# Normed rows through VectorE blocks and DRAM, LayerNorm sums on ScalarE, and masked blocks made differently, in a DeltaNet and Fourier-mixing kernel on one core

## The chip, the cores and the metric

The kernel runs on one core of a Trainium2 chip. Its time is the device time of one execution in microseconds. The median of the runs of the kernel before is 627.87 us. One execution was also taken by the hardware profiler, and every view of the profile below is of that one.

## The reference

Two blocks follow each other. The first is DeltaNet attention: four batches, eight heads, 768 tokens, head dimension 48, all float32. The second takes the heads side by side as 384 features, mixes tokens and features by two Fourier transforms, and adds a normalised two-layer network.

```python
k_n = k / (np.linalg.norm(k, axis=-1, keepdims=True) + 1e-06)
for t in range(S):
    y[:, :, t] = einsum('bhd,bhde->bhe', q[:, :, t], state)
    v_old = einsum('bhde,bhd->bhe', state, kt)
    state = state + bt * einsum('bhd,bhe->bhde', kt, vt - v_old)
x = y.transpose(0, 2, 1, 3).reshape(B, S, H * D)        # 4 x 768 x 384
u = x + real(fft(fft(x, axis=1), axis=2))
un = (u - mean(u)) / sqrt(var(u) + 1e-06)               # over the 384 features
out = u + maximum(un @ w_ch1, 0) @ w_ch2                # 384 -> 1536 -> 384
```

## The kernel before

**Attention.** The 24 units are pieces of 128 tokens of one batch (six to a batch, `T` = 0 to 5), each with all eight heads. Units are prepared in seven rounds. Rounds 0 and 1 (batch 0) go an early way of their own; the other five, of 4, 4, 4, 3 and 3 units, go through `prepare` and `consume`. For each unit TensorE turns keys and queries (`turn`, through line 353) and multiplies keys with keys and queries (`gram`). From the key products ScalarE and VectorE copy a diagonal part with a half mask into `lo` and join it with another part in `gd` (`ev_l`, `ev_g`, line 592). A round's `gd` is turned on VectorE into `rr` (line 643), inverted there row by row in sixty products and sums (`invert`, lines 936 and 941), scaled (line 950) and turned back (line 953). `blocks` then multiplies each unit's part of `gd` by a mask that keeps the upper triangle and the half it belongs to (line 963), turns 32-wide blocks (line 969), and the rest of the unit's inverse, its states and its outputs follow on TensorE (`quarters`, `ahead`, `step`, `outputs`).

**Mixing.** When a batch's six units are out, VectorE folds the rows (`folds`), TensorE does both transforms (`seq6`, `feat`), and VectorE adds and takes the LayerNorm statistics (lines 1515 and 1517). `normed` applies them to a 128 x 384 row tile `un` (VectorE, line 1539, or ScalarE, line 1537). There are six such tiles in a batch, two to a group `g`, twelve groups in all. Three TensorE transposes of 128 x 128 (line 353, tile `pm`) turn a tile, and one copy of 128 x 384 (line 359 on ScalarE or 361 on VectorE, `R<-pp`) brings it into `R0`, where the group's 256 tokens lie as [feature, token]. `R0` has places for two groups.

**Network.** `mlp` and `mlpw` read it from there as the moving operand of the first layer's products. `mlpw` uses a seven-product scheme for part of the work; its differences of 128 x 128 parts of the normed rows are made by VectorE at line 1728. Group (2,2) is worked in the last batch, after its attention.

**Order.** A string, `ORDER`, lists every piece of work in the order in which it is issued; each engine runs its own in that order. `issue` reads it. An entry has two characters for the piece, one for the engine if there is a choice, one for each new PSUM bank, and two more, for a DMA on SP with a size, that name the piece after which it is paced. An entry past the last piece is three characters: a group of dummy TensorE products (`fill`, lines 2172 and 2178). DMAs wait in SP's queue in the same manner: one that waits holds up those behind it.

```python
while place < len(text):
    i = take(2)
    if i >= len(self.ops):
        fill(i - len(self.ops), take(1))
        continue
    o, self.ins = self.ops[i], None
    e = o.engs[0] if len(o.engs) == 1 else ENGINES[take(1)]
    for b in o.new:
        b.slot = take(1)
    after = take(2) if o.kb and e == "SP" else i
```

Of the kernel before, what the change touches and what calls it, by code (L numbers as in the profile page):

```python
# [32 lines left out]
FOLD, SEQ, HOTG = 1, 10, 1  # L33
# [24 lines left out]
AGDAJDAKBAAAODAPBAEDARAWtGBAZAKAIDAMBAXAaAKABASACDAbGAAdCAcCAeBCAhGFAgBAfCAiANBA7AGAFBAUCA6A6AYAQBA4  # L58
AGATAjBMDBBNCAVAlAkAsAoADDAtBJEHBKCBLCAmAyAuAvGaAUAwBbA8ACA+CAxBPDEA9CA5AiBOCBQDCAQBCBCA2AzA0BmBnBqA
nBrBuBvA-FACoAGGbA0C8AFBRByApBzCzABBTB2CuAhDIAMAHDBACB3BBCBDA3C2A9B6A1ArB7HLBTBSAqBEBUHKBLtFHBVALDB+  # L60
BGtGHB-tGHBFCCtCHBHBaBWCDGjB-BIBcBdtGHBgCtAtCGBXBeCHBfDDFGCpDEGqAxDECCKtGCCqCCvCDDJABBhCLBiDKCBoCrHG
COGcBYBpCPCStGEBsCTG7DDC9EFBtGiBGCWtGABwCXHMBxtGACaB0CwCtGACbB1C+CCeCgCfCxABC0CB4DZCDXtGCDaCC3CDDcED
dDYCDeCCiB5ChDbCCsDfFDgHOGkC4CB8DhDjDiBZDkDlDmDFGHC5CDGmB9C6DoCCADpEDqDuCDNCpBjCBDtCDrCDsCDLCDDnCDvF
GzDjCyDwCEGrDgDxCDMC-ABCFCIDGCJCMDyCC1BDzCD0CD3GCD4CD1FED5CD6HDVDGD2CD7CD8DEGeD9CEAG6GmECCEDCEBFDEEG
yC0CNCQCRCUCVCYCZCcCdCjClCkEQCESCEOFRCETEERCEUEFCGdFTCFQEVCGfGgFVGC7CeCmFWEPCCnFUCFSBDBDBEWCEXEaEZEY
EbEcGsG8EdDABkEJFXCFYGELCEKCFZHDEBGhGlG0EMEgEGuENCEhEfCD+ABD-BGnGoFdDHDrG1FbEiCEwEkCElCFcFaFeFfEzCBl
EjCEGEeCGpDOBDPBEuCDEHCEIBEmEEvCEyCGtGvGwEnFiGFjFmBHSEDEpCEoCHTDAErCE2EqCEsABFkBExFEE0FnBG2E4CEtCE+A
BE1CFhBHCBkE5E7BE6BE8HUGdDQBFlCHVHVMYFcFgCHWHYHXHZE3CFoDE9CE-CFCHNFFCFECDRBHcEKFpMkBlG+G9G-FqBFtBHdE
kG3G4HAHfEvHPHQHaFDBCFGMLElFAFGFHCNJHEMKEsFLFBCFMBFrCFNCMIFbFsCFIFJCMZEoFOFPCFyFKCF0CGxFzEAHGHFFwFGH
eE2F1BHgF2FuBCHBF3CDSEoFxCMJFJHHHIHhHjFvCF4F6CG5HbF5CJNF7F8CDUEuF9CMlE7MmBDMoCF+GAFGF-CGEGFDCHiHkDTG  # L70
-JMGHBGBCMOFNMaFGMnCGGBMbCJOMwHhJPGIGCABGJCGDCGNGOCJQGKGPCHlJTJRHqF1JUHJHnFqHmHFGQHpHpH9FOMcCQPFLGRC
GLCJ3EFGMCGUGWCMpGHGVCHRJSJVGSABJWJZJcDWFsH1FNGTCH0JSJdJgMdCDMeJjHoHbHyHgQzJcMfGXHzMdHrFPMgM8GGJkGYC
GZCJ4MPMaJXJYJaJbJeJfJiJhMqH2JnH8GIJqHsMxGNJlJmJoH+MeHuJrIBJhMMJhJpJsJtHtMsHvHwH4M9JOJuBAJvJwJxCJyCM
jJ0CMiMhH3MrH5H6IAMaJ5J6CJ9CJ7BJ1CH-GVKADCKBJ8BHxKJAEMtKCKSGBMNF8QOJqJzCKKJ-CJ2CMvJ+BKDKTICMUGSKMKLM
yECH7KEKFM+DHNACIJIJM-CKNKbABIIJqKGMzCKHKVKOKcIKH2KIKPKkFDKtHEKeQbQbM0CKUKQKdKRIEKuM1BCK2IWJ4K3GIMIM
K5MuKWKlIDIFIGK4CM4K6AK7CIVMeILKIININIOQRMyKfKgKwNBDELHAIUKBM2QLIDIXK5KvIPM3KnIHNDKmQaM-KXM7IYIgKKNC
NEM6Q-Q-NGIQIRISIjKMNHLBGQyKCKYNINKIaIeKlLICNLIZKZIbIcLEFK8HITLFCM5NMNNIhM0NOQ0FANFNPIdQKM0IsM6KhK9C
KaNXLRItIDQcBCQeCIfIPQ2CIiKMIqIEIrKfNYNZNaNbNcNdK+HKoIkQ1CNRKiIlImInIoI3KeLKAKjKxKyKpK-CNeLADHLDKqI4
KlQ+NDIpLCCNfI5LHI2KhIuIZNgNhNiNjNkNlMVNCQdCNmNnKzNoIvK-NpJBJBLUI6LSFI8IwK0K1LTCQQIHQfBCQmIYJDJDIyQi
IxQhNqNrQnNqLGNsNQQNIbLVENtNuNvNwIzI0LJJAKpJEJEQgLLCQkNxI7RAAGNyI9I+QjNzLWCQMK1QoFEI1QlN0JFI9Q3BCRBC  # L80
I-LMQ7LXAN1N2N3N4Q4N5Q5Q8JCNRJGJHJJQ6QpCRLNSRCCN6KrKsJIJKJLLsQqCQrGFQvN7N8N9QsQuQtQwQxRDBCRGN+N-OARH
OBRERJOCLNLOLYCLZGQ9LbEFRFRIODRKOENVCMRLsRMOFRNROMSMSRPLaCLcBOGOHOILeRQOJOKLPMWQtRRMTMTRZRaOLOMLdCRb
ONRcRdOOReRfMQRAOPLhOQLfALtCRgLiBLgCOROSOTOUOVOwOWOxPOOXDOYCOyGLkNTCRhRiRjRkRlRmRnRoRpRqRrRsRtRuRvRw
RxOzCLjCLlAOZHO0BO2CPsLmCLnRyRzOcCRTOaCR0ObCOdCLuCR1MXMXO4CPPOeGAOfCDO3BPtPuHR2R3RUR4O1CR5R6R7R8PQBO
hCOiCPRBOjCOgCOkGLvLoNUCLpNWCLwAOlR9OmBCLqO5DEOnPvCLxCO6GHO9CO8COpFOoBOqO7CPSAR+R-SASBSCSDPWCPUCPwBO
-CDPTCPyCL0GO+CPAPCHPBCPVBOrADPzCPXFESEYiRTPxCL1CSFSGPDPEGHP0CYaOcPYBCOuQVPtPaCPbBOvSHSISJPGCPZCOtCL
yDQUOmLzCPFPHFPcCP1BCSKSLPJDGSMSNSOSPSQPISRSSSTP4CRSPdEFYjHBPNYbPQOsCPeP6CPfBYkCPgAPhP2EFYlCP5BPiABP
3CPMPjPLYtO-SUPkCYuHGYwCYvCLrPlCPKPmYmEFP7ABYxDCSVP8P+HYnYpP-YsYoP9CYzYqL2GHQSPLQTQTSWY0SXS1RVCQAABL
3ESYY1QBYyY2YrSZCYcP+QCCSaBS2PnFDPpRWBQFBCY4SWL4CZDPGQDAQESbEScBQIPoYdP7QJPqL5QGQHPrXhSeCSfCTSSdCY3S
gFESlCSjCShABY5CDSkBSiCY6BSmABY7CZEFEZFCSnSpCSoBS3DSqSrABZGCXiY8EFS4CStCS5CX8S8CY-SsY+ZHABX9TRZASuDZ  # L90
LSvS9CY9S7CZIZBS6BZPL8ZKTVZCZNTTS+DCZJS-ABTDCTBCTUXjEX+FZMQWY9ZOTACX-CXkCTEABTCCTFSwFCSxQZYySyTHETIT
GCTJABXlESzS0TKTLCTbYACTMFDTaTXTWTcTdTYYCCTQTPXnCL6ATOL9BXmCTNL7CYECTfTZTeThZQZRLQTkTgL-TiQYXlTjTnTq
TlTmTpTrXoCToTsTtL+CMCTuTvZSZTZUZVZdMADMBCZeZfMHTYT4AFZgQXQXZhZiRXCT5ZjT7BT9CTwBDZkXpCZXYDCT6CTxTzCT
yCZlT+CT1CT-BYBBXqEAT2CT0CZmZnZoXtCUKBDULUAFCYeMCZpZqXvCU9UBUUDEUMUNUOUCYfTuUDUVT3BT8CMDUeEFXrBCUPRY
CUEUWUFUXUQURXuCXwAUGUHMEUTMFUYUfZrUSXsCXxVIVJCUhUgZsUIZtUJYFFDYGGHYHCYJCXyBCVKEVEVLCUoAHYgMCZuYICVF
BZvUpVGGVHCUyEHVMGUZVAX0CVNCXzYKCZwZxU8ZyVSFZzVQVOZ0X3CBVPU+VTCUqUrUaUiUcVRVUX1DVCgMVIUjZ1X5CZ2UzUbV
WX4CUdVVVXZ3gSUTZ4UkZYU0Z5U-Z6Z7VDWEWFBX2U1Z8VYAHGVZFVaCVbZ9g1Z+VdUsVfVgCVhCVcZZCWGFZ-gzX6VeZaCaAUla
BVmVnEVkVoCVBaCX7ViVjaDaEVlVtYLDEaFaGaHaIaJWHCaKaLU2aMaNaOUmaPaQZWZbCVpVqYNCgTFCgUCVrUnYMVuBgVCVsaRa
SaTWIV0WJCWKFVvCaUaVVwVxWLCYOEgWBCgXaWaXaYaZYPVzgZVyYQEFYSCV2V1V4aaV5aba5a6YRWMDgaacbXV3a7EV9adFWNCY
VCDgYWOV7a8CYTEV8aeCYUWPafFagCa9BaiCV+a+CYWYYa-BahCYZajCYXWQWCV6gdgTWSEbABbBCakDFV-WAgNacbYgbapCWBWR  # L100
alCBamCbZHaqABWDWTBaoCanCarWUasCbCDFbGCbHCatCgeEGUtgfCauavABawbDEFggCaxBayCghABbFCbECaza0FCbIDEb1b2g
OV7gjbaBgla2a1UubJgkbbHgia4WYGAFbfCbKCgmbeBbdCWWWVgoVygpEDbLBa3gqBbcCbgHCgrCU3blCbMbkCgcgsDEgubNBCU4
U5gwWXgvgngtgygxg0g2WfUwbPCWZDWgEbjBg3g4g5bOWaCWbg6UvWcWhCbQBWdg7hCbhDCb3HbRhDYhg5bSEBMGWebWbiCb4CU6
# [2108 lines left out]
```

## Time and profile before

| | |
|---|---|
| runs | 625.07, 627.87, 3294.46 us; median 627.87 us |
| profiled execution | 629.74 us, its span 627.9 us |
| mean granted TensorE clock | 0.986 |
| TensorE busy | 603.0 us, 9722 products |
| VectorE busy | 533.7 us, 1477 instructions |
| ScalarE busy | 280.0 us, 790 instructions |
| DMA | 31.98 MB, mean 51 GB/s |

Busy time is a mean over stages. To about 100 us the attention of batch 0 is a chain of small steps beside the conversion of the weights; from then on attention of the next batch, mixing and network run beside each other, and from about 535 us only the network of the last batch is left. The 3294.46 us run is far from the other two, and the median doesn't feel it. Products overlap on TensorE, so the mean duration of one is longer than the time that it adds.

### The profile page before, as it was taken

The page shows a single profiled execution, that of the slowest core. Times are in us where ns is not written, and L with a number is a line of the kernel's source. Part 1 is how long each engine was busy: PE and PEld are TensorE (multiplying, and loading weights), DVE is VectorE, ACT ScalarE, POOL GpSimd, SP SyncE. Part 2 cuts the span into 40 slices and gives each one's busy share as a digit, 9 for nine tenths or more (in the row PEclk, how much of TensorE's full clock was granted, in tenths as well). Part 3 has the DMA queues.
Part 4 walks back from the last instruction along what each step waited for, and adds up shares of the span by engine and source line. Part 5 has one row for each costly group of instructions (what it writes and reads, how often), then busy time and mean ns, then how long its engine had stood idle before and what let it go on. Part 6 is the DMA issues. An engine that isn't in the chain of part 4 may idle for free.

```text
span 627.9 us, 22502 instructions
## 1 busy us (share of the span) xinstructions
PE 603.0 (96%) x9722; PEld 527.9 (84%) x9722; DVE 533.7 (85%) x1477; ACT 280.0 (45%) x790; POOL 30.8 (5%) x37
## 2 busy tenths in 40 slices
PE   6988889999989999999999999999999999999997
PEld 5678788867767777899889878789888889999997
DVE  5987889998978799899978999999986897877663
ACT  4778857535265452736353434513643213322210
POOL 2002412210000000000000000000000000000000
PEclk9979989999999898999999999999999999999999
DMA  6744535531004221210122030200100000100001
GB/s 136 204 114 124 129 94 144 134 86 39 2 2 92 52 56 58 37 27 2 29 54 64 16 64 1 52 2 14 41 3 4 3 26 1 51 2 1 26 2 50
DMA packets 85440, 31.98 MB, mean 51 GB/s; under 512 B 75996, under 2 KB 80829, under 8 KB 85341
## 3 DMA queue, kind: packets, MB, share of 16 engines
q1 hardware_dynamic: 85149, 30.31, 19.5%
q8 instruction: 76, 1.25, 0.8%
q10 hardware_dynamic: 192, 0.23, 0.1%
q14 instruction: 23, 0.19, 0.1%
HBM read 25.82 MB, written 4.72 MB: 49 GB/s over the span
## 4 chain that ended last, share of the span: by engine, by line
PE 88%; DVE 5%; ACT 3%; issue 2%; DMA 1%; POOL 1%; SPq 0%; DVEq 0%; ACTq 0%; POOLq 0%
PE pp L350 84%; PE pp L353 3%; PE pp L2178 1%; ACT us L359 1%; DMA us<-in_k_dram 1%; DVE x L1328 1%; PE pp L2172 0%; SPq L407 0%; DVE pm L1353 0%; DVE st L1291 0%; DVE x L1899 0%; DVE rr L689 0%; ACT pb L359 0%; DVE w L1975 0%; DVE gd L953 0%
## 5 line engine op out<-in xcount | busy, mean ns | idle before, releaser
L350 PE MATMUL pp<-R,w 128*128 128x256 f32 (+1 forms) x832 | 180.7, 367 | 0.7 <-DVE rr L941 0.7
L350 PEld LDWEIGHTS pp<-R,w 128*128 128x128 f32 x832 | 145.3, 191 | 19.6 <-DVE rr L941 0.8
L350 PE MATMUL pp<-us 64*64 64x64 f32 (+5 forms) x2704 | 94.2, 246 | 6.0 <-issue 3.0
L359 ACT ACTIVATE us<-pp 128x512 f32<-128x512 f32 (+4 forms) x153 | 59.4, 402 | 80.7 <-PE pp L350 53.4
L350 PE MATMUL pp<-w,R 128*128 128x384 f32 (+1 forms) x288 | 91.4, 442 | 0.0
L350 PEld LDWEIGHTS pp<-us 64*64 64x64 f32 (+3 forms) x2704 | 79.8, 145 | 12.3 <-issue 5.1
L350 PEld LDWEIGHTS pp<-w,R 128*128 128x128 f32 x288 | 51.4, 190 | 22.1 <-issue 0.3
L936 DVE TENSOR_TENSOR tmp<-rr 128x30 f32<-128x30 f32 (+9 forms) x150 | 49.6, 332 | 3.2
L941 DVE TENSOR_TENSOR rr<-rr,tmp 128x30 f32<-128x30 f32 (+9 forms) x150 | 48.9, 327 | 3.0
L350 PE MATMUL pp<-u,us 64*48 64x48 f32 (+2 forms) x1360 | 43.0, 222 | 5.0 <-DVE u L361 2.6
L350 PEld LDWEIGHTS pp<-u,us 64*64 64x64 f32 (+1 forms) x1360 | 36.7, 134 | 11.7 <-issue 5.0
L359 ACT ACTIVATE R<-pp 128x384 f32<-128x384 f32 (+8 forms) x66 | 26.9, 432 | 30.2 <-PE pp L353 14.7
L1795 DVE TENSOR_TENSOR us<-us,pp 128x256 f32<-128x256 f32 x64 | 26.2, 416 | 9.0 <-ACT us L359 6.0
L359 ACT ACTIVATE u<-pp 64x192 f32<-64x192 f32 (+1 forms) x65 | 21.2, 326 | 26.5 <-PE pp L350 24.0
L1830 ACT ACTIVATE R<-pp 128x512 f32<-128x512 f32 x21 | 12.5, 596 | 40.8 <-PE pp L350 35.1
L1607 ACT ACTIVATE R<-pp 128x512 f32<-128x512 f32 x24 | 14.1, 594 | 34.8 <-PE pp L350 34.8
L359 ACT ACTIVATE x<-pp 64x384 f32<-64x384 f32 (+2 forms) x44 | 18.3, 424 | 23.5 <-DVE u L1268 20.2
L350 PE MATMUL pp<-R,ws 128*128 128x192 f32 x144 | 27.9, 327 | 0.0
L350 PE MATMUL pp<-us,gd 128*128 128x192 f32 x144 | 27.5, 326 | 0.0
L359 ACT ACTIVATE us<-us,nr 128x48 f32<-128x48 f32 x112 | 26.4, 325 | 0.0
L350 PE MATMUL pp<-st,us 48*64 48x48 f32 (+1 forms) x1104 | 25.9, 223 | 0.5 <-issue 0.2
L1268 DVE TENSOR_TENSOR u<-u,pp 64x384 f32<-64x384 f32 x33 | 18.1, 548 | 9.4 <-PE pp L350 5.8
(206 smaller groups left out, 1076.1 us busy)
## 6 DMA issues: line engine op xcount, KB each, us to landing
out_dram<-x SPq DMA_DIRECT2D x11, 384.0 KB
us<-in_k_dram SPq DMA_DIRECT2D x16, 192.0 KB
us<-in_q_dram SPq DMA_DIRECT2D x16, 192.0 KB
us<-in_v_dram SPq DMA_DIRECT2D x16, 192.0 KB
x<-in_moe_w_ch_dram SPq DMA_DIRECT2D x11, 242.0 KB
R<-in_moe_w_ch_dram SPq DMA_DIRECT2D x8, 256.0 KB
ws<-in_moe_w_ch_dram SPq DMA_DIRECT2D x5, 242.0 KB
us<-in_q_dram SPq DMA_DIRECT2D x6, 181.5 KB
```

Of the source, the lines that this page charges most:

```text
L350: I(nc.tensor.matmul(o, lhsT=lhsT, rhs=rhs, start=start, stop=stop, skip_group_check=True))
L353: I(nc.tensor.matmul(o, lhsT=src, rhs=ident[p0:p0 + n, p0:p0 + n], is_transpose=True, start=start, stop=True, skip_group_check=True))
L359: I(nc.scalar.activation(o, i, ACT.Copy, **({} if scale is None else {"scale": scale})))
L936: I(eng(e).tensor_tensor(T_, R[:, :, j + 1:32, j:j + 1].broadcast_to([128, ns, n, j]), R[:, :, j:j + 1, 0:j].broadcast_to([128, ns, n, j]) ...
L941: I(eng(e).tensor_tensor(R[:, :, j + 1:32, 0:j], R[:, :, j + 1:32, 0:j], T_, op=ALU.add))
L1268: I(nc.vector.tensor_tensor(U, U, span(b1, 64 * c, 64 * c + 64, [[D, m], [1, D]], s0), op=ALU.subtract))
L1328: I(nc.vector.tensor_tensor(w, w, v, op=ALU.add))
L1607: I(nc.scalar.activation(o, s, ACT.Relu))
L1795: vec(256, lambda e: I(nc.vector.tensor_tensor(o, i0(), i1(), op=ALU.add)), [], [aH] + list(wr), pr - P.ev, use=n)
L1830: I(nc.scalar.activation(o, s, ACT.Relu))
L2178: I(nc.tensor.matmul(pst[x, 512 * bank:512 * bank + 256], lhsT=w[x, 0:128 // tiles], rhs=w[x, 0:256], start=True, stop=True, skip_group_ch ...
```

## The change

1. **Normed rows.** For eleven of the twelve groups (all but (0,0)) the three transposes and the copy from PSUM go. VectorE turns the 32 x 32 blocks of a tile, one DMA per tile writes it to a DRAM tile `zd`, and, once both tiles of the group are there, four DMAs read 32 partitions each back into `R0`. The rows then lie as eight runs of 32 tokens with 96 floats from run to run, and the network reads them so.
2. **LayerNorm sums.** For batches 1 to 3, `bn_stats` and `bn_aggr` on VectorE go; ScalarE sums with a copy and with a square (each over 128 x 384, with its accumulator), and the applied mean has its sign turned.
3. **Diagonal blocks.** For the 18 units of the five later rounds, the two masked copies to `lo` and the two joins at line 592 go; four copies of 32 partitions bring the diagonal blocks from PSUM to `gd`, each on ScalarE or VectorE. The triangle of the mask is now one product over the round's `gd` at the end of `invert`, and the masked product of `blocks` (line 963) becomes two scaled copies, each on ScalarE or VectorE.
4. **Order.** `ORDER` is another string: 7529 characters in place of 7307.

A function `turn_apart`, which would turn keys and queries in the same manner as the normed rows, is added for units from `APART` = 24 on; the units are 0 to 23, so it is not called.

```diff
-FOLD, SEQ, HOTG = 1, 10, 1
+FOLD, SEQ, HOTG, APART = 1, 10, 1, 24
...
-    m_k = pack[:, 192:256].rearrange("p (a t) -> p a t", a=2)
+    m_t = pack[:, 192:224]
... (gram)
-            for s in range(2):
-                def ev_l(e, s=s):
-                    t = psum(b[s]).rearrange("p (a j t) -> p a j t", a=2, j=NJ)
-                    copy(e, lo.rearrange("p (h t) -> p h t", h=H).rearrange(hs, s=2)[:, s],
-                         t[:, 1, :, 32 * s:32 + 32 * s], (m0, m1)[s])
...
+            for p0 in range(0, 128, 32):
+                def ev_d(e, p0=p0):
+                    copy(e, ro.gd(ul)[p0:p0 + 32].rearrange("p (j s t) -> p s j t", j=NJ, s=2),
+                         span(b, p0, p0 + 32, [[64, NJ], [1, 32]], 256 + p0 % 64))
+                P.op(either(256), ev_d, [], [A(gd0, g0, g0 + 256, p0, p0 + 32)], pr - P.ev, use=b, lat=LA)
...
-        for s in range(2) if not ro.early else ():
-            def ev_g(e, s=s):
-                I(nc.vector.scalar_tensor_tensor(w[0], w[1], (m1, m0)[s], w[2], op0=ALU.mult, op1=ALU.add))
... (invert, after the turn back)
+            x, n = ro.gd(0, len(ro.us)).rearrange("p (n t) -> p n t", t=32), 8 * len(ro.us)
+            vec(32 * n, lambda e, x=x, n=n: I(nc.vector.tensor_tensor(
+                x, x, m_t[:, None, :].broadcast_to([128, n, 32]), op=ALU.mult)), ...
... (blocks)
-        vec(512, f1, [ro.agd(ul), PK], [z.aTT()], pr, port=True)
+        for a in range(2):
+            def f1(e, a=a):
+                copy(e, z.TT[:, :, 32 * a:32 * a + 32], ro.gd(ul).rearrange(...), (m0, m1)[a])
+            P.op(either(256), f1, [ro.agd(ul), PK], [z.aTT(2 * a, 2 * a + 2)], pr, lat=LA, port=True)
... (feat, batches 1 to 3)
+            def total(e):
+                I(nc.scalar.activation(mx, u, ACT.Copy, accum_out=mv[:, 0:1]))
+            def squares(e):
+                I(nc.scalar.activation(mx, u, ACT.Square, bias=mv[:, 12:13], accum_out=mv[:, 1:2]))
... (normed)
+        if (b, g) != (0, 0):
+            def blockwise(e):
+                I(nc.vector.transpose(w.rearrange("p (c d k) -> p c d k", c=4, k=32),
+                                      un.rearrange("p (d c k) -> p c d k", c=4, k=32)))
+            def away(e):
+                I(nc.sync.dma_start(out=z[128 * tt:128 * tt + 128, :], in_=w))
+            def across(e):
+                for c in range(4):
+                    I(nc.sync.dma_start(
+                        out=ur[32 * c:32 * c + 32, uo:uo + 768].rearrange("p (a x) -> p a x", a=8),
+                        in_=z[:, 96 * c:96 * c + 96].rearrange("(a i) x -> i a x", i=32)))
... (mlp, mlpw)
-        un = ur[:, uo:uo + 768].rearrange("p (d n) -> p d n", d=KD)
+        un = ur[:, uo:uo + 768].rearrange("p (n d k) -> p d n k", n=8, d=KD)
```

More of the change, by code (lines that the diff above doesn't have):

```diff
@@ L63 @@
[L63 to L67, printed above, removed]
@@ L2081, in prepare @@
             load(z, "q")
-            turn(z, 0)
+            (turn_apart if z.u >= APART else turn)(z, 0)
             gram(z, ro, i, 0)
```

262 lines of the change are left out of this document (152 added, 110 removed).

## The prediction

> **What bounds the kernel now.** I read the busy time by stages first, then the chain that ended last, and only then the groups of instructions. The stages, cut where the page's forty slices change (columns: stretch, its length, then busy time of PE, PEld, DVE, ACT and POOL, the granted clock, the DMA share and GB/s):
>
> ```profile
> 0.00:100.00 100.00, 85.58 (x2193) 75.75 (x2194) 83.15 (x240) 67.94 (x177) 19.10 (x28) 0.95 0.55 135
> 100.00:175.00 75.00, 74.78 (x690) 57.12 (x689) 71.36 (x194) 35.89 (x95) 11.04 (x8) 1.00 0.29 72
> 175.00:250.00 75.00, 69.51 (x1821) 55.04 (x1809) 63.04 (x156) 38.04 (x113) 0.31 (x1) 0.95 0.23 54
> 250.00:622.00 372.00, 371.11 (x5031) 338.29 (x5030) 313.55 (x884) 138.17 (x406) 0.31 (x1) 1.00 0.09 22
> 622.00:628.00 6.00, 2.02 (x13) 1.72 (x11) 2.60 (x7) 0.00 (x0) 0.00 (x0) 1.00 0.35 131
> ```
>
> TensorE is without a gap from 250 to 622 us (371.11 of 372.00) and all but without one from 100 to 175. It has 5.49 us of gaps between 175 and 250, and there its clock is 0.95 as well. VectorE is 95% busy in the second row (71.36 of 75.00) and 84% in the fourth: close behind. ScalarE has room everywhere but in the first 100 us.
>
> The chain, in order of time (start, length, what), says the same of the long stage, and shows what a transposed tile costs in it:
>
> ```profile
> 138.92 26.60 PE pp L350 x184
> 165.52 0.33 PE pp L353 x3
> 165.84 14.29 PE pp L350 x265
> ...
> 480.36 54.02 PE pp L350 x686
> 534.39 0.66 PE pp L353 x6
> 535.04 25.30 PE pp L350 x188
> ```
>
> Three transposes (line 353, `pm`) take 0.33 us from the end of the product before to their own end, six take 0.66. Nothing waits ahead of or behind them: each tile's 0.33 us is a piece of the path.
>
> Between 209 and 225 us the chain leaves TensorE, and runs along VectorE, instruction on instruction:
>
> ```profile
> 209.92 0.34 DVE gd L592
> 210.86 1.88 DVE gd L953
> 212.76 0.76 DVE R L963 x2
> ...
> 215.60 0.61 DVE gd L592 x2
> ...
> 221.09 0.69 DVE us L963
> 222.25 0.26 DVE gd L592
> ```
>
> This is batch 1's first round, and VectorE's list is what TensorE waits for. Six of the instructions listed here (three of line 592, three of line 963) are of kinds that the change takes away.
>
> **The change part by part.** The profiled execution took 629.74 us, 1.84 more than its span. The rows of the groups that are touched (count, then total busy us and mean ns; the second row has min/median/max ns and the first and last start):
>
> ```profile
> L353 PE MATMUL pp<-pack,pm 128*128 128x128 f32 x72 | 10.9, 274 | 0.0
> L353 PE MATMUL pp<-pack,pm x72: 270/273/329, 106.6 to 588.3; 128*128 128x128 f32 x72
> L359 ACT ACTIVATE R<-pp 128x384 f32<-128x384 f32 x20 | 9.6, 489 | 14.9 <-PE pp L353 14.7
> L969 DVE STREAM_TRANSPOSE t<-us 128x256 f32<-128x256 f32 x16 | 6.8, 431 | 0.3 <-PE pp L350 0.2
> L953 DVE STREAM_TRANSPOSE gd<-rr 128x1024 f32<-128x1024 f32 x5 | 9.8, 1968 | 0.1
> L1515 DVE BATCH_NORM_STATS2 mv<-x 128x6 f32<-128x384 f32 x24 | 13.2, 553 | 0.2
> L1517 DVE BATCH_NORM_AGGREGATE mv<-mv 128x2 f32<-128x6 f32 x24 | 4.1, 174 | 0.1
> L592 DVE SCALAR_TENSOR_TENSOR gd<-us,pack,lo 128x128 f32<-128x128 f32 x32 | 11.5, 382 | 0.5 <-ACT us L359 0.4
> L963 DVE TENSOR_TENSOR us<-gd,pack 128x512 f32<-128x512 f32 x16 | 10.6, 676 | 0.2
> L950 DVE TENSOR_TENSOR rr<-rr,gb 128x1024 f32<-128x1024 f32 x5 | 6.1, 1220 | 0.1
> L359 ACT ACTIVATE lo<-pp,pack 128x128 f32<-128x128 f32 x36 | 12.1, 365 | 7.6 <-DVE us L573 3.8 <-PE pp L350 2.9 <-DVE gd L592 0.9
> L1537 ACT ACTIVATE pm<-x,mv 128x384 f32<-128x384 f32 x11 | 7.8, 707 | 0.3
> ```
>
> *Transposes off TensorE.* 22 of the 24 tiles change, 66 products. By the chain that is 22 x 0.33 = **7.3 us**; by the group's busy time 66 of 72 times 10.9, or 10.0. They start between 106.6 and 588.3 us, where TensorE has hardly a gap but in the third stage. I take 7.3; the ends are nothing (TensorE waits for the tile instead) and 10.0.
>
> *Blocks on VectorE.* A 128 x 384 block transpose isn't in the trace. The 128 x 256 one with runs of 32 takes 0.43 us, the 128 x 1024 one with scattered writes 1.97; at the rate of either, 384 elements take 0.65 or 0.74. I take 0.65, since here too both sides move in runs of 32. That is 14.3 us of VectorE for 22 tiles.
>
> The Trainium skill ("VectorE: DVE Perf Modes", section "Rules for kernel authors") says to give a 128 x 128 transpose to TensorE where PSUM will do as its destination. The rows agree as far as engine time goes: 0.33 us of TensorE against 0.65 of VectorE. By that rule the edit is the wrong way round, which is the third case below.
>
> *VectorE's and ScalarE's sums.* VectorE loses 18 x (0.553 + 0.174) = 13.1 us of statistics, 36 x 0.382 = 13.8 of line 592, 18 x 0.676 = 12.2 of line 963: 39.1. It gains 14.3 of blocks and five triangle products, the size of line 950's in four-unit rounds and three quarters of it in the others, 3 x 1.22 + 2 x 0.92 = 5.5. The 72 diagonal copies and the 36 scaled copies may go to either engine; at the 0.365 of the copies to `lo` that is 39 us, of which VectorE could take all or none. So its balance is between -19 and +20, with an even split about 0. ScalarE loses 36 x 0.365 = 13.1 and some 9 of evictions, and gains two passes of 128 x 384 for each of 18 tiles, at 0.49 (the PSUM copy of that size) to 0.71 (line 1537) 18 to 26 us. Its busy time in the stages' rows is 280 us of 628: it isn't a bound. Its cover in the long stage is TensorE's queue; without that, the statistics would be late by 2 x 0.6 - 0.73 = 0.5 us a tile. I put nothing in the sum for either engine in the long stage.
>
> In the VectorE stretch from 209 to 225 us it counts: 0.34 + 0.61 + 0.26 and 0.76 + 0.69 are 2.7 us taken from the path, and the round's triangle product (1.22) is put on it right after line 953. The copies in their place can go to ScalarE, 51% busy in that stage. I take **1.4 us** gained. The ends are a loss of 1.2 (all copies on VectorE) and 5.5, all of TensorE's gaps in the stage.
>
> *The way through DRAM.* A tile is now ready after blocks, a DMA out and, with its partner's, four DMAs in. A load that ended a wait, and the issue on SP's queue (min/median/max ns):
>
> ```profile
> 96.93 1.93 DMA us<-in_k_dram
> L1572 SPq DMA_DIRECT2D out_dram<-x x13: 350/383/578, 199.7 to 624.9; - x13
> ```
>
> One leg out: 0.38 + 1.93 = 2.3 us. Four issues and a landing back: 1.5 + 1.93 = 3.4. With 0.65 of blocks 6.4 us, in place of 0.33 + 0.49 = 0.8 for transposes and copy. So each of eleven groups is ready about **5.6 us** later than today. The string can put other work between. Groups with g = 1 and 2 come while the group before is being worked on, 25.30 us by the chain's last row above. The starts of batches 1 and 2 have the next batch's attention beside them. The start of batch 3 has least:
>
> ```profile
> 534.23 0.82 PE L353 MATMUL pp<-pack,pm 128*128 128x128 f32 x6
> 535.53 1.03 PE L350 MATMUL pp<-ft,R 97*128 97x97 f32 x8
> 536.32 0.30 PEld L350 LDWEIGHTS pp<-R,w 128*128 128x128 f32 x2
> ```
>
> Six transposes, and 2 us later the first product that reads them, with a tile of `feat` and a little of group (2,2) between. More of (2,2) would have to be kept for it. I put **1 us** of loss there; the ends are nothing and 5.6.
>
> *SP's queue.* 22 writes and 44 reads are put among the loads: 66 x 0.38 = 25 us of issuing in 400. Each write waits for VectorE, each read for its write, so loads and stores behind them wait some 3 to 6 us a group. What covers this is that loads sit in the queue for buffers anyway:
>
> ```profile
> SPq L407 <- PE pp L350: 148.0, 28, 32.1
> ```
>
> 28 waits on TensorE alone come to 148 us, 5 us each, and after 100 us no load stands on the chain. Nothing in the sum; uncovered it would be the second case's.
>
> *Strided moving operand.* The rows are now read in runs of 32 floats, 96 floats from run to run. Products of which the second half of an inverse (`TT[:, :, 32:64]`) is the operand already read two such runs, `pb` below; `lo` reads one piece:
>
> ```profile
> 31.03 1.15 PE L350 MATMUL pp<-lo,w 64*64 64x64 f32 x32
> 56.03 1.13 PE L350 MATMUL pp<-us,pb 64*64 64x64 f32 x32
> L350 PE MATMUL pp<-R,w 128*128 128x256 f32 x704 | 165.4, 384 | 0.7 <-DVE rr L941 0.7
> ```
>
> 1.13 against 1.15 us for 32: no price. But these are small, and the 704 that will read that way are not; each tenth on them is 16.5 us. I take nothing.
>
> *The order.* The string is 222 characters longer. The pieces account for 22 x 2 + 22 x 4 + 11 x 4 - 22 x 6 = 44 for the rows, 18 x 4 for the diagonal copies, 18 x 4 for the scaled ones and 5 x 2 for the triangle, 198 together. The other 24 are eight more groups of dummy products (three characters each). Today's groups stand at 3 to 31 us, where nothing else can run:
>
> ```profile
> L2178 PE MATMUL pp<-pack x24: 379/483/793, 2.9 to 30.3; 128*128 128x256 f32 x20, 64*64 64x256 f32 x4
> L2172 PE MATMUL pp<-pb x36: 222/222/369, 20.7 to 23.2; 128*64 128x64 f32 x36
> ```
>
> Eight more at one or two of 0.38 to 0.48 us each are 3 to 8 us of TensorE; in gaps they cost nothing, and I take that. What else a new order does in the first 100 us I can't read; I give it 3 us either way.
>
> The sum: 629.74 - 7.3 - 1.4 + 1.0 = 622.0 us for a twin of the profiled execution. That one is 1.87 above the median, so against 627.87 I forecast 627.87 - 7.7 = **620 us**, 1.2% less.
>
> **The rivals.** *First, more than the sum.* The third stage's gaps (5.5 us) and its clock (5% of 75 us, 3.7) both come back with a lighter VectorE, beside 7.3 to 10.0: 16.5 to 19 us, 609 to 611. For it speaks the stretch of VectorE on the chain; against it that the balance of VectorE is about even, and that the new triangle product stands in that very stretch. *Second, slower: the way through DRAM isn't covered.* Then TensorE stands still at the head of a group for up to 5.6 us. Three batch starts cost 16.8, which gives 627.87 - 8.7 + 16.8 = 636; all eleven give 62 and 681. It decides from the second uncovered group on (8.7 by 5.6). For it: today's first products follow within 2 us of a batch's first transposes. Against: work of another batch lies beside all but the last start. *Third, nothing gained: VectorE becomes the bound.* Its load goes up by as much as 20 us if the copies land there, and between 100 and 175 us it has 3.6 us to spare; then the 7.3 us come back as waits, 626 to 630. For it 71.36 of 75.00; against it ScalarE's room. *Fourth, the strided read costs a tenth or two:* 620 + 16.5 to 33, 637 to 653.
>
> **How the numbers follow.** The forecast (615.3 to 626) has 0.55, more than the sum 0.17, VectorE as the bound 0.13, uncovered groups 0.12, the strided read 0.03. A measurement of this kernel can tell about 2% from no change, 12.6 us: below 615.3 counts as faster, above 640.4 as slower. Faster gets 0.17; slower half of the uncovered case and the strided one, 0.09; the rest 0.74. The range goes from 611, where the first rival's sum begins, to 630, the end of the third. It leaves out the slow two and a little of the fast one, under 0.2.
>
> **What would show it.** Right: no line 353 on `pm` but two tiles' six; TensorE still without a gap from 250 us to the end, its busy time 4 to 10 us less; VectorE's total within 15 us of today's 533.7; block transposes of 0.55 to 0.75 us; the products that read the rows (x704) at the same 165 us. The second rival would show as waits of TensorE on a DMA into `R0` at heads of groups, the third as waits on VectorE in the long stage, the first as fewer gaps and a clock nearer to 1.00 between 175 and 250 us. My forecast is wrong if the first 100 us move by more than 3 us, which I can't see from here, or if the dummy products stand in full stages.

## The result: 1% slower, and where the profile shows it

The changed kernel takes **630.6 us** (median of 11 runs), the kernel before 625.1 us beside it: a ratio of 1.010, 95% interval 1.0068 to 1.0131. A second series gave 630.7 against 624.9 us, 1.010 with 1.0057 to 1.0144. The forecast was 620 us, 1.2% less, in a range from 611 to 630; the change went the other way.

The stages of the changed kernel, cut as those of before (stretch, length, busy time of PE, PEld, DVE, ACT, POOL, granted clock, DMA share, GB/s):

```profile
0.00:100.00 100.00, 85.67 (x2233) 76.53 (x2234) 83.81 (x253) 74.45 (x190) 19.83 (x30) 0.95 0.55 139
100.00:175.00 75.00, 73.09 (x682) 54.82 (x681) 69.93 (x182) 41.44 (x110) 10.14 (x7) 1.00 0.32 83
175.00:250.00 75.00, 72.90 (x1737) 57.51 (x1735) 65.89 (x165) 40.22 (x113) 0.31 (x1) 1.00 0.26 61
250.00:622.00 372.00, 365.23 (x5020) 330.43 (x5021) 310.34 (x859) 151.96 (x440) 0.31 (x1) 0.99 0.16 42
```

In the long stage TensorE now has 6.8 us of gaps, where it had 0.9. But the two profiles end at the same time (spans 627.3 and 627.9), although the medians are 5.5 us apart, so a stage-by-stage comparison of these two misleads. The kernel before, profiled a second time, shows why. Spans and mean granted clocks, first of that second profile, then of the changed kernel's two:

```profile
core 0: 621.3 us, clock 1.000
```
```profile
core 0: 627.3 us, clock 0.985
```
```profile
core 0: 628.8 us, clock 0.983
```

The execution from which the prediction was worked out (629.74 us, clock 0.986) was one of the slowest of its kernel. At 1.000 the same program takes 623.1 us. The changed kernel has to be laid beside this second profile.

One product marks batch 3's last attention being over: the first of `tab,R` on all 97 rows (`x48`). Its start (first column), in the timelines of the second profile of before, of the changed kernel and of its second profile:

```profile
512.97 5.03 PE L350 MATMUL pp<-tab,R 128*97 128x65 f32 x48
```
```profile
512.94 5.12 PE L355 MATMUL pp<-tab,R 128*97 128x65 f32 x48 [0.21 <-DVE R L1377]
```
```profile
514.41 5.12 PE L355 MATMUL pp<-tab,R 128*97 128x65 f32 x48 [0.20 <-DVE R L1377]
```

From there to the end of the span it is 108.3 us in both profiles of the kernel before (519.63 to 627.9 in the first) and 114.4 in both of the changed one. **Six microseconds are lost in the last batch's start; up to there the change has brought nothing,** although 16 of the 22 tiles lie before that point. Where their gain went can be told in part. From the first normed tile (103.11 us in the second profile of before, 102.27 in the changed kernel) to the marking product the granted clock is 1.00 in both, and they take 409.9 and 410.7 us. Sixteen tiles at 0.33 us would be 5.3 us less. Late groups of dummy products take 3.6 us there (experiment 2), and one stop, on a weight conversion of VectorE, is new:

```profile
139.39 1.56 PE L355 MATMUL pp<-w,R 128*128 128x384 f32 x4 [1.77 <-DVE w L2038]
```

These two come to 5.4 us, about the gain that was expected; but without the dummy groups the time didn't fall either, as will be seen.

What stands in the lost stretch is one stop of TensorE (timeline; in brackets how long it was idle and what ended it), and the granted clock behind it (stretches of 5 us, columns as above):

```profile
534.97 1.17 PE L355 MATMUL pp<-ft,R 95*128 95x97 f32 x4 [3.67 <-DVE x L1962]
535.93 1.33 PE L355 MATMUL pp<-R,w 128*128 128x128 f32 x5
```
```profile
530.00:535.00 5.00, 1.33 (x11) 1.17 (x9) 4.82 (x15) 3.01 (x12) 0.00 (x0) 0.88 0.25 59
535.00:540.00 5.00, 5.00 (x21) 4.82 (x22) 2.19 (x8) 0.51 (x2) 0.00 (x0) 0.50 0.00 0
540.00:545.00 5.00, 5.00 (x41) 4.90 (x40) 2.95 (x7) 1.95 (x6) 0.00 (x0) 0.94 0.01 3
```

TensorE waits 3.67 us, and then works at half clock: 0.6 + 2.5 + 0.3, or 3.4 us of full clock, are withheld over 15 us. The Trainium skill ("TensorE: Matmul & The Clock Gate", section "What's actually happening") says that the clock goes to one half after an idle window of about 3.4 us; this stop agrees.

The chain of waits ahead of that product (start, length, what) runs along ScalarE's new sums and VectorE:

```profile
529.77 0.63 ACT eo L1549 x2
...
530.74 0.72 ACT eo L1555 x2
...
532.25 0.37 DVE u L1962
...
533.23 0.83 DVE x L1962 x2
...
534.97 5.06 PE pp L355 x20
```

Lines 1549 and 1555 are the two summing passes of the LayerNorm, line 1962 the last sums of group (2,2). Feature tile 5 of batch 3 needs the PSUM bank that these sums hold; VectorE comes to them late, and TensorE's next work, the first products of (3,0), is queued behind that tile.

### The profile page after: what moved, and what is told of

It is laid out like the page before. It is cut to its first block, busy times and chain, and to the rows that moved or that the text cites. A ratio compares the mean times of both kernels' runs of the same rounds, so it can differ in the third digit from the quotient of the medians.

```text
span 627.3 us, 22553 instructions
## 1 busy us (share of the span) xinstructions
PE 598.4 (95%) x9674; PEld 520.5 (83%) x9674; DVE 532.2 (85%) x1460; ACT 308.1 (49%) x851; POOL 30.6 (5%) x39
## 4 chain that ended last, share of the span: by engine, by line
PE 78%; DVE 12%; ACT 5%; issue 2%; DMA 1%; POOL 0%; DVEq 0%; SPq 0%; ACTq 0%; POOLq 0%
PE pp L355 75%; ACT us L364 2%; PE pp L358 2%; PE pp L2241 1%; DVE R L1377 1%; DVE x L1962 1%; DVE us L607 1%; DVE w L2038 1%; DVE pm L1377 1%; ACT R L364 1%; PE pp L2235 1%; DMA us<-in_q_dram 1%; DVE x L1352 1%; DVE u L1292 1%; DMA R<-in_k_dram 1%
## 5 line engine op out<-in xcount | busy, mean ns | idle before, releaser
L355 PE MATMUL pp<-us 64*64 64x64 f32 (+6 forms) x2704 | 92.0, 236 | 12.0 <-ACT us L364 9.3
L355 PEld LDWEIGHTS pp<-us 64*64 64x64 f32 (+3 forms) x2704 | 76.9, 137 | 20.2 <-ACT us L364 12.9
L364 ACT ACTIVATE us<-pp 32x128 f32<-32x128 f32 (+4 forms) x149 | 57.9, 404 | 63.8 <-PE pp L355 39.3
L964 DVE TENSOR_TENSOR rr<-rr,tmp 128x30 f32<-128x30 f32 (+10 forms) x150 | 51.0, 340 | 3.1
L959 DVE TENSOR_TENSOR tmp<-rr 128x30 f32<-128x30 f32 (+10 forms) x150 | 48.9, 327 | 3.3
L355 PE MATMUL pp<-u,us 64*48 64x48 f32 (+2 forms) x1360 | 39.4, 216 | 0.2
L1893 ACT ACTIVATE R<-pp 128x512 f32<-128x512 f32 x20 | 12.0, 598 | 40.0 <-PE pp L355 36.0
L364 ACT ACTIVATE gd<-pp 32x256 f32<-32x256 f32 x65 | 23.8, 374 | 15.4 <-PE pp L355 4.8
L355 PE MATMUL pp<-ft,R 97*128 97x97 f32 (+1 forms) x192 | 26.4, 283 | 4.6 <-DVE x L1962 3.7
L355 PEld LDWEIGHTS pp<-ft,R 97*128 97x128 f32 (+1 forms) x192 | 23.8, 193 | 6.6 <-DVE x L1962 3.8
```

Of the source, the lines that this page charges most:

```text
L355: I(nc.tensor.matmul(o, lhsT=lhsT, rhs=rhs, start=start, stop=stop, skip_group_check=True))
L364: I(nc.scalar.activation(o, i, ACT.Copy, **({} if scale is None else {"scale": scale})))
L959: I(eng(e).tensor_tensor(T_, R[:, :, j + 1:32, j:j + 1].broadcast_to([128, ns, n, j]), R[:, :, j:j + 1, 0:j].broadcast_to([128, ns, n, j]) ...
L964: I(eng(e).tensor_tensor(R[:, :, j + 1:32, 0:j], R[:, :, j + 1:32, 0:j], T_, op=ALU.add))
L1893: I(nc.scalar.activation(o, s, ACT.Relu))
```

## The experiments

**1. The parts without the order, and the order without the parts.** Each part got a flag. Its pieces stand in the old string where the pieces that they replace stood (for `none_new` the other way round).

```diff
+ROWS, SUMS, DIAG = 1, 1, 1     # all_old; rows_old 1,0,0; sums_old 0,1,0; diag_old 0,0,1; none_new 0,0,0
-        if (b, g) != (0, 0):
+        if ROWS and (b, g) != (0, 0):
...
-        if b == 0:
+        if b == 0 or not SUMS:
...
+            if not DIAG:           # masked copies to lo, joins, masked product as before
```

> All three parts, in the order of before: each new piece stands where the piece that it replaces stood (or just ahead of the first that needs it). If the new order is what costs (six late groups of dummy products, 3.7 us on the chain; the stop of 3.7 us at 531 us and the clock of 0.86 beside it), this one keeps the 7.3 us of transposes and comes to about 617 us, unless the starts of the batches, with nothing put between, stop TensorE for up to 5.6 us each: then 617 to 634. If the parts themselves cost, in VectorE's list or on the way through DRAM, it is slower than both, 635 or more.

> None of the three parts, in the order of after. If the order costs: after plus the 7.3 us of transposes, 636 to 640 us. If the parts cost and the order is as good as the old one: 622 to 627, like before.

> The normed rows by VectorE blocks and DRAM alone, in the order of before; sums and diagonal blocks as before. Covered everywhere: 625 - 7.3 = 618 us. With three uncovered batch starts at up to 5.6 us: 618 to 634. If each of eleven groups stops TensorE: above 640.

> The LayerNorm sums on ScalarE alone, in the order of before. VectorE is 13 us lighter, ScalarE 18 to 26 us heavier. If neither is on the path: 624 to 626 us. If the longer chain of the sums holds up the start of the last batch: 1 to 3 us more than before.

> The kernel before with the third part of the change alone (diagonal blocks copied straight, one triangle product, two scaled copies), in the old order with the new pieces in the places of the old ones: copies to lo become copies on ScalarE, the joins become copies on VectorE. The prediction's term for the VectorE stretch from 209 to 225 us was a gain of 1.4 us, ends -1.2 and 5.5. Theory A (it is a trade of like for like on engines with room): 621 to 627 against 625. Theory B (like the other two parts it fits only an order made for it): 630 or more.

| kernel | us | ratio to before, 95% |
|---|---|---|
| all three, old order | 713.5 | 1.137 (1.128 to 1.147) |
| none, new order | 681.7 | 1.089 (1.081 to 1.096) |
| rows alone, old order | 680.8 | 1.089 (1.083 to 1.096) |
| sums alone, old order | 643.8 | 1.028 (1.022 to 1.035) |
| diagonal blocks alone, old order | 652.8 | 1.048 (1.042 to 1.054) |

Parts and order fit only each other. That all three, the rows and the diagonal blocks could be slow in the old order was among what was expected (635 or more, above 640, 630 or more); 643.8 for the sums and 681.7 for none lie outside everything that was. What TensorE waited for (total us, times, longest), and the longest such stop, in rows alone; then in sums alone; then in diagonal blocks alone:

```profile
PE pp L358 <- DMA R<-zd: 32.1, 8, 12.2
```
```profile
431.69 4.88 PE L358 MATMUL pp<-R,w 128*128 128x256 f32 x12 [12.24 <-DMA R<-zd]
```
```profile
409.68 5.46 PE L358 MATMUL pp<-R,w 128*128 128x256 f32 x12 [4.47 <-ACT R L367]
```
```profile
PE pp L359 <- DVE gd L370: 14.7, 8, 4.1
```

The rows wait for DRAM, at heads of groups; in the 12.24 us stop the second tile's blocks are made at 425.21, written at 425.84 and read from 427.79 us on. The sums wait for ScalarE. The diagonal copies, put on VectorE where the joins stood, take 0.42 us each and are waited for. The second rival's price for a way through DRAM without cover at any head was 62 us; rows alone cost 56, but that the two are so near is luck: the waits on `R<-zd` come to 32.1 us at eight heads, 6.1 more are a wait on a load, and a granted clock of 0.957 withholds some 29 of 679 us. In the new order the list of what TensorE waits for, down to 0.2 us, has no DMA into `R0`: there it is hidden.

**2. The late dummy groups, and the start of batch 3.** Six of the 20 groups now stand late, five pieces of the chain:

```profile
216.87 0.63 PE pp L2241 x2
...
227.17 0.63 PE pp L2241 x2
...
228.67 0.63 PE pp L2241 x2
...
252.09 1.21 PE pp L2241 x6
...
255.04 0.46 PE pp L2241 x2
```

```diff
 # no_late_dummies (and both_mended)
-fill x6, after the pieces of 216 to 255 us
 # batch3_start (and both_mended): entries of ORDER around feature tile 5 of batch 3
-PE  feat (3, T=5), banks 4, 2
+PE  feat (3, T=5), banks 4, 7
+ACT minus, squares, root (3, T=2); ss (3, T=4)        # ahead of total (3, T=3)
+DVE recip (3, T=2); g2, g1 (3, T=4)                   # ahead of the weight differences (line 1765)
+SP  away, across (3, T=1)                             # ahead of feat (3, T=4)
+DVE row differences of (3,0)                          # ahead of the last sums of (2,2)
```

> The changed kernel without the six late dummy groups (those of its trace at 216.87, 227.17, 228.67, 252.09 and 255.04 us); all else as it is. Theory A (the dummies stand on the path, because the stage is full): the time falls by their rows, 0.63 + 0.63 + 0.63 + 1.21 + 0.46 = 3.6 us, from 630.6 to about 627.0, and the granted clock stays near 0.985. Theory B (they fill waits that would be there anyway): within 1 us of 630.6. Theory C (a pause there lowers the granted clock): 630 or more, with a clock under 1.00 between 200 and 275 us.

> The changed kernel with the start of batch 3 put in another order: feature tile 5 takes a bank that is free, feature tile 4 is evicted and tile 2's squares are summed ahead of the weight differences, and the row differences of (3,0) go ahead of the last sums of (2,2). Theory A (the 3.67 us stop of TensorE at 531.3 us is the one that costs, and the clock of 0.86 from 525 to 550 us follows from it): the stop falls to under 1 us and the clock there returns to 1.00; the stop is worth 2.7 to 3.7 us and the clock 25 us x 0.14 = 3.5 us, so 623.5 to 625 instead of 630.6. Theory B (VectorE's chain sets this stretch whatever the order): the stop moves to the first products of (3,0) with the same length, and the time stays within 1 us of 630.6. Theory C (the stop goes, the clock does not come back): 627 to 628.

> Both edits: no late dummy groups and the new start of batch 3. If both theories A hold the gains add: 630.6 - 3.6 - 6 = 621, 3 to 4 us below the kernel before (624.5). If the dummies only fill waits: 624 to 625, level with it. If neither holds: 630.

> The kernel before, unchanged, for a second profile. The profile that the prediction used ran 629.74 us at a granted clock of 0.986; seven other runs of it lay at 622.5 to 629.6 with clocks of 0.988 to 0.998. If the prediction's sum began from an execution with more throttled slices than usual: this one lies at 622 to 625 us with a clock of 0.995 or more, the stages after 200 us at 1.00, and the difference to 629.74 is the clock (627.9 x 0.986 = 619.1 us of full clock against about 621 x 0.997 = 619.1). If the clock does not decide: another time at the same clock, or the same time at another clock.

> The changed kernel as it is, a second profile. Theory A (the loss lies after the last transform of batch 3, in the stop and the clock fall): from the first tab,R product of batch 3 to the end again 113.5 to 115 us, against 108.3 in the kernel before and 109.7 to 109.8 in the two kernels with a mended start; the stop again 3.67 us. What lies before that product moves with the clock of the first 60 us, by up to 6 us. The time 629 to 632, ratio 1.007 to 1.013. Theory B (one execution's chance): another length after it, 110 to 112.

Without the late groups: 632.6 us, ratio 1.0144 (1.0111 to 1.0177), so not faster at all. Its profile has a clock fall where the groups had been:

```profile
230.00:235.00 5.00, 3.32 (x148) 2.92 (x144) 3.67 (x9) 1.87 (x5) 0.00 (x0) 0.89 0.02 3
235.00:240.00 5.00, 5.00 (x27) 4.20 (x21) 4.88 (x16) 1.36 (x5) 0.00 (x0) 0.76 0.60 174
```

With the start of batch 3 mended: 626.4 us, ratio 1.0063 (1.0031 to 1.0095). Against the changed kernel's 1.0100 that is 0.37%, 2.3 us, and from the two intervals uncertain by 0.45%, so by itself not clear of noise. With both edits: 628.8, ratio 1.0088 (1.0057 to 1.0118), 0.56% or 3.5 us less than without the groups alone, which is beyond the uncertainty. The profiles say it more sharply: the long stop is gone and the clock behind it stays up. From the marking product to the end it is 628.0 - 518.2 = 109.8 us in batch3_start:

```profile
518.20 1.74 PE L355 MATMUL pp<-tab,R 128*97 128x65 f32 x15 [0.21 <-DVE R L1377]
```
```profile
537.59 1.34 PE L355 MATMUL pp<-R,w 128*128 128x128 f32 x8 [0.59 <-DMA R<-zd]
```
```profile
525.00:550.00 25.00, 23.01 (x170) 22.07 (x170) 22.25 (x62) 12.53 (x44) 0.00 (x0) 1.00 0.13 41
```

So the mended start gives back 4.6 of the 6.1 us lost there, less than the 5.6 to 7.1 that were expected of the stop and its clock fall together. The wait for the way through DRAM is 0.59 us of the rest.

**3. The transposes by themselves,** in the kernel before. Theirs was the term of 7.3 us.

```diff
-            for dt in range(KD):
+            for dt in range(KD if (b, T) in ((0, 0), (0, 1)) else 0):                        # before_no_transposes
...
+                    tr(psum(bk)[:, 128*dt:128*dt+32], un[0:32, 128*dt:128*dt+128], 0, 32, dt == 0)  # thin_transposes
```

> The kernel before without 66 of its 72 transposes of normed rows on TensorE (those of all tiles but the first two); their evictions stay and copy what the bank held, so the output is not the reference's. Prices the first term of the prediction's sum by itself: 7.3 us by the chain of waits (22 tiles of 0.33 us), ends 0 and 10.0. If the term is right and the clock stays as in before: 623.8 - 7.3 = 616.5 (613.8 to 619 taken as agreeing). If TensorE only waits elsewhere instead: 621 to 624. If the gaps that come of it lower the clock: 620 or more with a clock under 0.99.

> The kernel before, whose 66 transposes of normed rows (all tiles but the first two) turn 32 rows instead of 128: as many instructions of TensorE in the same places, a quarter of the columns moved; the output is not the reference's. Saves at most three quarters of 7.3 us, 5.5; by the weight loads that remain (each still 128 columns) rather half, 3.6. Theory A (the removal of instructions shifts where TensorE stops without a shown cause, and that ate the gain of before_no_transposes): such stops stay at about 4 us and the time is 619 to 621.5 against 624.1. Theory B (the transposes stood beside other waits): 623 to 625, as without them.

Without 66 transposes the kernel before takes 623.5 us against 624.1: ratio 0.9988 (0.9956 to 1.0021), a gain of 0.6 us, at most 2.7. Taking them away shows in the stops that have no shown cause ("issue"; total, times, longest), first in the second profile of before, then without transposes; then the one at 459 us, and stretches of 5 us around it and around another at 183 us:

```profile
PE pp L350 <- issue: 4.2, 9, 1.1
```
```profile
PE pp L350 <- issue: 6.8, 8, 2.0
```
```profile
459.32 0.25 PE L350 MATMUL pp<-pb,t 64*32 64x32 f32 x4 [1.62 <-issue]
```
```profile
180.00:185.00 5.00, 3.02 (x151) 2.77 (x143) 3.42 (x9) 2.44 (x9) 0.00 (x0) 0.81 0.03 7
185.00:190.00 5.00, 5.00 (x18) 3.87 (x12) 1.80 (x5) 1.19 (x4) 0.00 (x0) 0.51 0.00 0
455.00:460.00 5.00, 3.38 (x153) 3.07 (x153) 3.64 (x9) 2.01 (x8) 0.00 (x0) 0.95 0.02 3
460.00:465.00 5.00, 5.00 (x92) 4.91 (x93) 2.52 (x6) 1.46 (x6) 0.00 (x0) 0.71 0.01 3
```

In this profile 2.6 us of such stops are new, and the clock falls behind two of them (rows 1 and 2, rows 3 and 4) withhold 3.4 and 1.7 us. Together that is 7.7 us, as much as the term. Over many runs it looks much the same: a straight line of time against granted clock, laid through the 23 runs of the kernel before and the 12 without transposes, puts the latter 2.3 us lower at the same clock, uncertain by 0.9, and their clock is lower (median 0.993 against 0.997). By this estimate, which is no experiment on the clock, a third of the term is there, and most of that third goes back through the clock. Whether the stops come because instructions are fewer isn't settled. The other kernel was to say so, and can't: thin transposes save too little (chain, six of them):

```profile
352.90 0.48 PE pp L353 x6
```

That is 0.48 against 0.66 us for six, and 0.30 against 0.33 for three, so 0.7 to 2.0 us for 22 tiles. Its 625.5 us against 625.2 (1.0023, 0.9989 to 1.0057) is too small a test.

**4. The first 60 us.** There the changed kernel has pauses of TensorE on ScalarE, and half clock behind them:

```profile
12.42 1.16 PE L355 MATMUL pp<-us 48*64 48x64 f32 x62 [2.46 <-ACT us L364]
25.84 1.16 PE L355 MATMUL pp<-us 48*64 48x64 f32 x64 [1.61 <-ACT us L364]
28.83 1.02 PE L355 MATMUL pp<-us 48*64 48x64 f32 x27 [1.82 <-ACT us L364]
```
```profile
15.00:20.00 5.00, 5.00 (x67) 3.75 (x60) 4.51 (x11) 2.49 (x6) 0.00 (x0) 0.67 1.02 292
30.00:35.00 5.00, 5.00 (x70) 4.11 (x68) 1.91 (x4) 2.98 (x12) 0.00 (x0) 0.50 0.02 7
```

```diff
 # all start from batch3_start
+fill x3 ahead of keys (block 4)                              # early_dummies, first_pause
+fill x2 ahead of gram (block 0), x2 ahead of gram (block 1)  # early_dummies; x2 and x1 in evictions_two
+ACT turn/ev (block 5) x2, ahead of begin16 (lines 719, 721)  # early_evictions, evictions_two, evictions_more
+ACT turn (blocks 1, 4, 2), ahead of scaled copies            # evictions_more
 # from the kernel before
-fill x12                                                     # before_no_dummies
```

> The kernel batch3_start with seven more dummy groups, 3 in the pause of TensorE at 9.96 to 12.72 us, 2 in that at 26.9 to 28.51 and 2 in that at 29.8 to 31.46. More work for TensorE and nothing else. Theory A (the granted clock falls to one half for some 7 us after a pause of 1.5 to 2.5 us in a stretch with little work, and each such fall costs about 3.4 us of full clock, most of it on the path): the three falls between 10 and 55 us go, the profiled clock is 0.995 or more, and the time falls from 626.4 to 620 to 623. Theory B (the early falls lie beside waits for VectorE and ScalarE and cost nothing): the clock rises and the time stays within 1 us of 626.4. Theory C (the pauses do not set the clock): the falls stay, and the time rises by up to 4 us, what the seven groups take.

> The kernel batch3_start with 3 dummy groups in the first pause alone (9.96 to 12.72 us). Theory A (the clock falls cost, and early_dummies lost its lead by stops that have nothing to do with the first pause): the fall at 12 to 23 us goes, those at 30 and 47 us stay or go with it, and the time is 622 to 625 against 626.4. Theory B (each dummy group on the path costs, or an earlier start moves the later work into stops): 627 to 632, as early_dummies.

> The kernel batch3_start with the two evictions of key block 5's transposes put ahead of the four ScalarE instructions of the first inverse (norm, root, two copies) that stand before them; no dummy groups added. The pause of 2.46 us at 12.72 us shrinks to under 1 us. Theory A (clock): the first fall, 12 to 23 us, goes; 2 to 4 us less than 626.4, so 622.5 to 624.5. Theory B (the inverse's chain on VectorE and ScalarE sets the first 60 us): the norm starts some 1.2 us later, and the time is 626 to 628 whatever the clock does.

> The kernel early_evictions with 2 dummy groups in the pause ahead of 26.96 us and 1 in that ahead of 29.93 us. Theory A (clock): the two falls after 27 us go, the clock rises from 0.989 to 0.995, and the time falls from 624.9 to 620 to 622.5, below both kernels. Theory B (the dummies stand on ScalarE's and VectorE's path, or move code to other places): 626 to 632.

> The kernel early_evictions with three more evictions of transposes (blocks 1, 4 and 2 of the query and key turns) ahead of scaled copies on ScalarE's list; nothing added. The pauses of 1.61 us at 26.96 us and of 1.30 us at 29.93 us should fall under 0.8 us. Theory A (a pause is worth its length and its clock fall): 621 to 623 against 624.9. Theory B (these pauses stand beside the inverse's own chain): 624 to 626.

> The kernel before without its twelve dummy groups, all of which stand at 3 to 31 us. Theory A (they hold the granted clock up): the profile shows falls to one half in the first 60 us, a clock of 0.97 to 0.99, and the time rises by 2 to 6 us from 623.8. Theory B (they only take TensorE's time): the clock stays at 0.995 or more and the time falls by 0 to 3 us.

| kernel | us | ratio to before, 95% |
|---|---|---|
| early_dummies (7 groups) | 632.7 | 1.0138 (1.0091 to 1.0185) |
| first_pause (3 groups) | 629.8 | 1.0064 (1.0032 to 1.0095) |
| early_evictions | 624.9 | 1.0014 (0.9985 to 1.0044) |
| evictions_two (3 groups) | 628.1 | 1.0039 (1.0012 to 1.0066) |
| evictions_more | 627.4 | 1.0034 (1.0002 to 1.0067) |
| before_no_dummies | 630.4 | 1.0107 (1.0067 to 1.0148) |

The clock alone doesn't decide here. Seven groups bring the profiled clock to

```profile
core 0: 627.5 us, clock 0.997
```

and the time up: by the ratios 0.75%, 4.7 us, over batch3_start, uncertain by 0.57%. That profile is 7.9 us ahead of batch3_start at the first normed tile (99.39 against 107.25 us) and 0.4 ahead at the marking product (517.77 against 518.20): stops without a shown cause and one more clock fall, 1.89 us of stop at 438.73, take part of the lead, and the rest isn't accounted for. With three groups the clock stays at 1.00 from 10 to 25 us, where it had fallen, and by the ratio nothing is gained (1.0064 against 1.0063). My reading, which no run here tests by itself: a clock fall beside a wait for ScalarE is free, and dummy work ahead of a late product isn't. Yet the kernel before loses 6 us without its groups, so it isn't a rule; nor do they work as was expected, for its profile without them has no clock fall before 80 us.

Two evictions moved ahead, which add nothing, fared best: level with the kernel before. They are the best of five tries, and the way in which they were to help didn't come: the pause shrank from 2.46 to 1.46 us, not under 1, and the fall behind it stayed in the profiles of all three kernels that have this edit. With more evictions moved, the pauses at 27 and 30 us grew to 1.96 and 1.98 us instead of falling under 0.8, and the fall behind them stayed too (evictions_more):

```profile
15.00:20.00 5.00, 5.00 (x45) 3.16 (x35) 4.90 (x16) 2.37 (x5) 0.00 (x0) 0.66 0.92 242
30.00:35.00 5.00, 4.72 (x66) 3.98 (x66) 2.86 (x5) 3.76 (x15) 0.00 (x0) 0.50 0.01 3
```

Why early_evictions gains is therefore open. No version was faster than the kernel before.

## Why the prediction was wrong, step by step

- **Transposes off TensorE, -7.3 us: the step that failed.** The term was mis-sized: 0.6 us measured, 2.7 by the far end of the interval. The reading behind it was that nothing waits ahead of or behind the transposes, so that each tile's 0.33 us is a piece of the path. A piece of the chain tells what TensorE did, and not what goes away with it: in the profile without them 2.6 us of new stops and 5.1 us of withheld clock stand in their place. Why these come stays open. Of the ends given, "nothing" was the nearer one, though for another reason (TensorE was to wait for the tile).
- **The way through DRAM, +1 at the start of batch 3.** The start costs 6.1 us, beyond the end of 5.6, and by another mechanism: not the DMA (no wait in the changed kernel, 0.59 us with the start mended) but ScalarE's sums and VectorE's late sums, on which a bank waits. The step that called VectorE and ScalarE nothing in the long stage failed at this one place. "Late by 0.5 us a tile" was in it; "its cover is TensorE's queue" didn't hold where the next product stands behind the late one. Of the rivals the third comes nearest (626 to 630 us, a wait on VectorE in the long stage), but VectorE didn't become the bound: its load is as before.
- **VectorE's stretch in batch 1's first round, -1.4.** Gaps of the third stage fell to 2.1 us, from 3.5 in the second profile of before (71.46 of 75.00 busy), but 1.9 us of the busy time are the first three late dummy groups. Net nothing. The clock of 0.95 in that stage, on which the first rival counted, was that one execution's.
- **Dummy groups.** Eight more, as counted, and six stand in full stages, which the prediction named as a sign of its failure. The sign came, and 3.6 us of the chain are theirs; but without them a clock fall takes their place, and nothing is gained.
- **What held.** TensorE's busy time fell by 4.6 us (603.0 to 598.4), as forecast, but by luck: it is 597.3 in the second profile of before. VectorE's total is 532.2 us (533.7 before). The strided read has no price: the 704 products take 165.0 us, 164.7 in the second profile of before. Blocks take 0.57 us where 0.65 was taken:

```profile
L355 PE MATMUL pp<-R,w 128*128 128x256 f32 x704 | 165.0, 384 | 0.0
```
```profile
L1591 DVE STREAM_TRANSPOSE tv<-pm x11: 555/571/580, 111.1 to 575.6; 128x384 f32<-128x384 f32 x11
```

- **The base.** The forecast was set against 627.87, a median of three with a profile at clock 0.986. Series of the kernel before have since lain at 623.8 to 625.5. The same sum from there gives 617, further from what came.

In sum, by the ratios: 1.0100 as changed, 1.0063 with the start of batch 3 mended, 1.0014 with two evictions moved ahead as well (the last step 0.49%, uncertain by 0.44%, and picked from five). What is left can't be told from nothing. One loss is traced to its cause, the order at the start of batch 3; that the first 60 us are the second is likely and not shown. The gain to be set against them was small from the start: 0.6 us without the transposes, and at most 2.7.

## What to carry to other kernels

Price an operation that leaves a busy engine by leaving it out, not by its piece of the chain: 66 transposes that filled 7.3 us of the chain were worth 0.6, at most 2.7. Look at the granted clock of a profiled execution before you sum from it, and lay profiles beside each other between products that mark the same point, not in fixed stretches. An order written out for a set of pieces is a part of their cost: each of three parts alone was 3 to 9% slower in the old one, and the search for a loss begins at the starts of stages, where one bank held by a late sum stops everything behind it.

## What the runs showed of the hardware

The granted clock falls to one half also after pauses shorter than the 3.67 us one. In the changed kernel it does so after 2.46 us, ahead of the row at 15 us (1.7 us of full clock withheld), and after 1.61 and 1.82 us, ahead of that at 30 us (0.86, 0.50 and 0.96 in the rows from 25 to 40 us, so 3.4 us withheld), both in stretches of small products. The Trainium skill ("TensorE: Matmul & The Clock Gate", section "HAM oscillation — how this bites in real kernels") gives the rule to leave no idle gap above about 3.4 us; by these rows it doesn't keep products this small safe. The length of the pause doesn't decide alone. In the first profile of before the clock is 0.50 from 40 to 45 us with no pause longer than 0.8 us in the 10 us ahead, and in that of before_no_dummies it stays at 1.00 over 2.41 us:

```profile
23.83 1.11 PE L352 MATMUL pp<-pack,us 64*128 64x64 f32 x15 [2.41 <-ACT us L358]
20.00:25.00 5.00, 1.65 (x24) 1.23 (x24) 4.96 (x18) 2.98 (x9) 0.00 (x0) 1.00 0.90 242
```

What else decides, no run here shows. ScalarE's sums each carry a second instruction that reads the accumulator:

```profile
L1549 ACT ACTIVATE eo<-x x18: 507/522/526, 252.3 to 562.7; 128x384 f32<-128x384 f32 x18
L1549 ACT ACTIVATION_READ_ACCUMULATOR eo<-x x18: 184/186/193, 252.7 to 563.2; 128x1 f32 x18
```

That is 0.19 us on top of 0.52, and on top of 0.62 in the second pass, so two passes take 1.5 us a tile where VectorE's statistics took 0.73. Three transposes on TensorE, after other products, hardly get shorter with 32 rows turned in place of 128: 0.30 against 0.33 us. Six in a row do: 0.48 against 0.66.
